# Three weight loads moved ahead of the last wait of a decode kernel

## The chip, the cores and the metric

The kernel runs on one core of a Trainium2 chip. The metric is the device time of one execution in microseconds (us); a profile's span is 2.0 to 2.6 us shorter than that time. PE is TensorE, the matrix engine; PEld are the weight loads (LDWEIGHTS) that the program has for its matmuls; ACT is ScalarE and DVE is VectorE. PSUM is where the program keeps the buffers that its matmuls write (`pm_r` here). Engines signal each other through semaphores. A ratio is the mean time of one kernel's runs over the mean of the other's runs of the same rounds, so it is not quite the ratio of the medians quoted beside it.

## The reference, cut to what matters

One token goes through an attention block over a cache of 65,536 keys and an MLP; both results and the token are added.

```python
xn = _layernorm(A_x)
return A_x + _A_ref(xn, A_k_cache, A_v_cache, A_wq, A_wo) + _B_ref(xn, B_w1, B_w2, B_w3, B_w4)
# _B_ref ends with:  h2 = _gelu(_layernorm(x1) @ w3) @ w4;  return x1 + h2      (w4: 3584 x 1024)
```

About 170 MB of caches and weights are read (169.87 MB on the page) for a result of 1024 numbers. The product with w4 comes last.

## The kernel before

Nearly all data come through one queue (169.87 of 170.03 MB), w4 last; its last four pieces get smaller (11, 5, 2 and 1 rows for each partition). So the last piece is one row of w4 for each partition. Its product is split over four column strips of the PE array (`tile_position=(0, 32 * q)`): two halves j of the result times two halves h of each. So one "row" is four weight loads and four matmuls of 256 columns. Strips 0 and 1 go to one PSUM buffer, read by ACT; strips 2 and 3 to another, read by DVE.

```python
    def narrow_rows(lo, hi):
        wt = st.tiles["w4"]
        for c in range(lo, hi):
            for h in range(2):
                for j in range(2):
                    q = 2 * h + j
                    nc.tensor.matmul(quarters[h][32 * q:32 * q + 32, 0:256], lhsT=hT[:, c:c + 1].to_broadcast([P, 32]),
                                     rhs=wt[:, D * c + 512 * j + 256 * h:D * c + 512 * j + 256 * (h + 1)], start=False, stop=False,
                                     tile_position=(0, 32 * q), skip_group_check=True)
    # ... (cut)
    nc.scalar.copy(out=out_t[:, 0, :], in_=quarters[0][0:64, 0:256])
    nc.vector.tensor_tensor(out=out_t[:, 1, :], in0=quarters[1][64:128, 0:256], in1=sums[1][:], op=ALU.add)
    nc.scalar.dma_start(out=out[0, 0, :].rearrange("(j n) -> j n", j=2), in_=out_t[31:33].rearrange("p h n -> p (h n)"))
```

On PE the last row stands as load 1, matmul 1 (waits for the last piece), load 2, matmul 2, load 3, matmul 3, load 4, matmul 4. Only matmul 1 has a wait.

Of the kernel before, what the change touches and what calls it, by code (L numbers as in the profile page):

```python
# [15 lines left out]
P = 128  # L16
# [12 lines left out]
def keep_loaded_weights(nc):  # L29




    for function in nc.m.functions:
        for block in function.blocks:
            held, kept = {}, []
            pe = [i for i in block.instructions if i.engine == mybir.EngineType.PE]
            user = dict(zip((i.name for i in pe), pe[1:]))
            for i in block.instructions:
                if i.engine == mybir.EngineType.PE:  # L40
                    if i.opcode == "Ldweights":
                        what = (i.tile_size, str(i.ins[0]))
                        waits = [j for j in (i, user[i.name]) if j.sync_info is not None and j.sync_info.on_wait]
                        if waits:
                            held.clear()
                        elif held.get(i.tile_position) == what and i.sync_info is None:
                            continue
                        if any(size != i.tile_size for size, _ in held.values()):
                            held.clear()
                        held[i.tile_position] = what  # L50
                    elif i.opcode != "Matmult" or i.ldweights is not False:
                        held.clear()
                kept.append(i)
            block.instructions = kept


# [41 lines left out]
def kernel(  # L98
# [13 lines left out]
):  # L112
    nc = tc.nc
    nc.at_finalize(keep_loaded_weights)
    nc.at_finalize(lead_with_the_first_load)
    nc.at_finalize(close_on_the_store)
    D = A_x.shape[-1]
# [413 lines left out]
    sums = [ogpool.tile([64, 256], F32, name="sums_a", tag="og"), ppool.tile([64, 256], F32, name="sums_b", tag="p")]  # L531
# [62 lines left out]
```

## Time and profile before

| | before |
|---|---|
| time, median of 3 runs (range) | 400.79 us (400.72 to 401.16) |
| span of the profiled execution | 398.6 us |
| end of the last transfer in the chain | 396.45 us |
| first matmul of the last row | 396.50 us |
| start of DVE's closing addition | 396.86 us |
| issue of the store | 397.36 us |

Everything the change can win lies between 396.50 and 396.86 us.

### The profile page before, as it was taken

To read this page: it belongs to the slowest core of one execution; us is meant where nothing else is said; L and a number is where in the kernel's file an instruction comes from. 1 tells how busy PE (TensorE), PEld (TensorE's weight loads), DVE (VectorE), ACT (ScalarE), POOL (GpSimd) and SP (SyncE) were. 2 spreads that over 40 slices of the span, in tenths; PEclk is the share of its full clock that TensorE was granted. 3 is DMA by queue.
4 is the path that set the end of the run, shared out by engine and by line. 5 is a ranking of instruction groups with operands and counts; after the bars stand their busy time and mean duration, and the time that the engine had idled before them with its cause. 6 is when DMAs were issued, how large, how long until landed. Compare 5 with 4: busy or idle time off the path is not lost.

```text
span 398.6 us, 2623 instructions
## 1 busy us (share of the span) xinstructions
PE 230.2 (58%) x1372; PEld 45.2 (11%) x862; DVE 211.5 (53%) x162; ACT 27.8 (7%) x36; POOL 10.0 (3%) x38
## 2 busy tenths in 40 slices
PE   0272970591569247834964297429553946394986
PEld 0210010000200010011001100101010102010142
DVE  0602010965196559643963696269449932894141
ACT  1002010003000200020002000200110020002000
POOL 2100000000000000000000000000000000002000
PEclk9998896697659686966895679678966986599999
DMA  9998999999999999999999999999999999999996
GB/s 421 421 443 382 439 441 480 434 427 421 416 428 427 434 460 442 427 427 421 427 429 427 467 434 434 423 421 427 441 429 441 454 427 388 418 455 431 409 427 260
DMA packets 4310, 170.03 MB, mean 427 GB/s; under 512 B 457, under 2 KB 459, under 8 KB 844
## 3 DMA queue, kind: packets, MB, share of 16 engines
q1 hardware_dynamic: 4294, 169.87, 98.9%
q8 instruction: 9, 0.15, 0.2%
q14 instruction: 1, 0.01, 0.0%
q10 hardware_dynamic: 6, 0.00, 0.0%
HBM read 169.87 MB, written 0.00 MB: 426 GB/s over the span
## 4 chain that ended last, share of the span: by engine, by line
DMA 54%; DVE 21%; PE 18%; ACT 2%; another core or an unknown queue 2%; SPq 1%; POOLq 1%; issue 1%; DVEq 0%; ACTq 0%
DMA big<-in_A_k_cache_dram 41%; DVE big L387 15%; PE sc L392 11%; DMA big<-in_B_w_dram 7%; DMA big<-in_A_wq_dram 6%; PE oacc L442 4%; DVE p_sb L413 2%; DVE mx L397 2%; PE psq L307 2%; ACT p_sb L410 2%; SPq L194 1%; POOLq L589 1%; ACT L410 0%; PE pm_mx L399 0%
## 5 line engine op out<-in xcount | busy, mean ns | idle before, releaser
L392 PE MATMUL sc<-big,qdiag 128*128 128x512 bf16 x512 | 128.5, 411 | 65.8 <-DVE big L387 65.6
L387 DVE STREAM_TRANSPOSE big<-big 128x4096 f32<-128x4096 f32 x32 | 139.4, 4412 | 48.0 <-DMA big<-in_A_k_cache_dram 48.0
L442 PE MATMUL oacc<-big,p_sb 128*32 128x512 bf16 x512 | 44.0, 520 | 34.5 <-DVE p_sb L413 34.5
L397 DVE TENSOR_REDUCE mx<-sc 128x1 f32<-128x2048 f32 x8 | 18.3, 2291 | 29.7 <-PE sc L392 29.7
L392 PEld LDWEIGHTS <-qdiag 128*128 128x128 bf16 x128 | 13.1, 102 | 176.6 <-issue 145.2
L410 ACT ACTIVATE p_sb<-sc,nball 128x2048 bf16<-128x2048 f32 x8 | 15.7, 1967 | 219.4 <-DVE nball L408 219.4
L413 DVE STREAM_TRANSPOSE p_sb<-p_sb 128x2048 bf16<-128x2048 bf16 x8 | 18.5, 2311 | 18.0 <-ACT p_sb L410 18.0
L442 PEld LDWEIGHTS <-p_sb 128*32 128x32 bf16 x512 | 16.8, 126 | 59.1 <-DVE p_sb L413 35.1
L451 DVE SCALAR_TENSOR_TENSOR og<-oacc,wb,og 128x512 f32<-128x512 f32 x4 | 3.0, 750 | 28.7 <-PE oacc L442 28.7
L307 PE MATMUL psh<-big,ln_rep_b 128*32 128x512 bf16 (+1 forms) x64 | 12.4, 942 | 4.0 <-DMA big<-in_B_w_dram 4.0
L485 PE MATMUL o_acc<-big,oT 128*1 128x512 bf16 x48 | 11.9, 413 | 2.4 <-ACT p_sb L410 2.4
L399 PE MATMUL pm_mx<-ident_f,mx 128*1 128x128 f32 x8 | 2.3, 283 | 19.1 <-DVE mx L397 19.1
L307 PE MATMUL psq<-big,ln_rep_a 128*32 128x512 bf16 x64 | 8.9, 445 | 4.1 <-DMA big<-in_A_wq_dram 4.1
L348 DVE STREAM_TRANSPOSE h_row<-h_row 128x896 bf16<-128x896 bf16 x1 | 1.1, 1111 | 17.2 <-ACT h_row L347 17.2
L332 POOL COPY qdiag<-qx 32x32 bf16<-32x32 bf16 x16 | 3.2, 203 | 262.8 <-PE sc L392 246.0
L250 PE MATMUL pm_ln<-ln_rowsum_a,ones_f 128*128 128x1 f32 x2 | 0.6, 348 | 12.5 <-DVE ln_rowsum_a L248 12.5
L320 DVE CAST q_row<-psq 64x1024 bf16<-64x1024 f32 x1 | 1.2, 1217 | 11.9 <-PE psq L307 11.9
L236 PE MATMUL psB<-big,hT 128*32 128x512 bf16 x46 | 5.5, 380 | 2.6 <-DMA big<-in_B_w_dram 2.6
L241 DVE STREAM_TRANSPOSE x_t<-x_row 32x256 bf16<-32x256 bf16 x4 | 2.5, 615 | 8.1 <-DMA x_row<-in_A_x_dram 8.0
L464 PE MATMUL pm_e<-ol,sel8big 128*128 128x129 f32 x6 | 1.8, 385 | 7.9 <-DVE ol L462 7.9
L406 PE MATMUL pm_mx<-ident_f,rep 1*128 1x1 f32 x8 | 1.9, 234 | 5.0 <-DVE rep L403 5.0
L448 ACT COPY og<-oacc 128x512 f32<-128x512 f32 x4 | 2.3, 585 | 33.5 <-PE oacc L442 24.4
(112 smaller groups left out, 77.1 us busy)
## 6 DMA issues: line engine op xcount, KB each, us to landing
big<-in_A_wo_dram SPq DMA_DIRECT2D x1, 8192.0 KB
big<-in_B_w_dram SPq DMA_DIRECT2D x1, 7168.0 KB
big<-in_B_w_dram SPq DMA_DIRECT2D x3, 2048.0 KB
big<-in_B_w_dram SPq DMA_DIRECT2D x1, 2816.0 KB
big<-in_B_w_dram SPq DMA_DIRECT2D x1, 1280.0 KB
big<-in_B_w_dram SPq DMA_DIRECT2D x1, 512.0 KB
big<-in_B_w_dram SPq DMA_DIRECT2D x1, 256.0 KB
big<-in_A_k_cache_dram SPq DMA_DIRECT2D x8
```

Of the source, the lines that this page charges most:

```text
L194: go(out=t[i0:i0 + 4 * k:4, WHOLE * D:(WHOLE + m) * D].rearrange("e (i n) -> e i n", i=m), in_=w4_v[m0:m0 + k * m, WHOLE, :].rearrange("(i ...
L236: return nc.tensor.matmul(psB[32 * j:32 * j + 32, :], lhsT=lhsT.to_broadcast([lhsT.shape[0], 32]), rhs=rhs, start=start, stop=False, tile_ ...
L307: nc.tensor.matmul(acc[32 * q:32 * q + 32, i, 0:n], lhsT=rep[:, c, :], rhs=cols(c, i, q), start=(c == 0), stop=(c == DC - 1), tile_positio ...
L332: nc.gpsimd.tensor_copy(out=qdiag[at, LEAD:].rearrange("p (x c) -> p x c", x=4)[:, :, 32 * a:32 * a + 8], in_=qx[at, :, 8 * g:8 * g + 8])
L387: nc.vector.transpose(out=words, in_=words)
L392: nc.tensor.matmul(sc[:, e, :], lhsT=qdiag[:, c0:c0 + P], rhs=cols[:, s, e, :, b2, :, r], start=(s == 0 and b2 == 0 and r == 0), stop=(s = ...
L397: nc.vector.reduce_max(out=mx[:], in_=sc[:].rearrange("p e n -> p (e n)"), axis=AX.X)
L410: nc.scalar.activation(out=p_sb[:], in_=sc[:], func=ACTF.Exp, bias=nball[:, b:b + 1], scale=SCALE, accum_out=group["lall"][:, b:b + 1])
L413: nc.vector.transpose(out=flat, in_=flat)
L442: mm = nc.tensor.matmul(oacc[32 * q:32 * (q + 1), :], lhsT=pT[:, e, 32 * t:32 * (t + 1)], rhs=vt[:, :, e, t, :], start=(e == 0 and t < 4), ...
L485: nc.tensor.matmul(tail["rows"][0:1, h2, :], lhsT=oT[g][:, j:j + 1], rhs=wt[:, g, j, 512 * h2:512 * (h2 + 1)], start=(g == 0 and j == 0), ...
L589: with _tile.TileContext(nc) as tc:
```

## The change

Its intent: have the weights of the last row in the array when its data land, so that nothing but the matmuls is left to do then. It edits the finished list of instructions: the loads of matmuls 2, 3 and 4 are put ahead of matmul 1. The other engines' instructions stay as they were.

```diff
+def load_last_row_ahead(nc):
+    for function in nc.m.functions:
+        for block in function.blocks:
+            pe = [i for i in block.instructions if i.engine == mybir.EngineType.PE and i.opcode in ("Ldweights", "Matmult")]
+            if len(pe) < 8:
+                continue
+            row = pe[-8:]
+            loads, sums = row[::2], row[1::2]
             ... (three assertions cut)
+            moved = {i.name for i in loads[1:]}
+            kept = []
+            for i in block.instructions:
+                if i.name == sums[0].name:
+                    kept += loads[1:]
+                if i.name not in moved:
+                    kept.append(i)
+            block.instructions = kept
...
     nc.at_finalize(keep_loaded_weights)
+    nc.at_finalize(load_last_row_ahead)
```

More of the change, by code (lines that the diff above doesn't have):

```diff
@@ L53, in keep_loaded_weights @@
                 kept.append(i)
+            block.instructions = kept
[7 more added lines that the diff above has]
+            loads, sums = row[::2], row[1::2]
+            assert all(i.opcode == "Ldweights" and i.sync_info is None for i in loads)
+            assert all(i.opcode == "Matmult" and i.tile_size == (P, 32) for i in sums)
+            assert sorted(i.tile_position for i in loads) == [(0, 32 * q) for q in range(4)]
+            moved = {i.name for i in loads[1:]}
[5 more added lines that the diff above has]
+                    kept.append(i)
             block.instructions = kept
```

## The prediction

The forecast's sum came to 12 ns, from 282.5 - 270.5 ns, with a range of 9 to 17. An allowance for PE's queue went into the upper end: it was not worked out from a trace. "Computed end" is the end of a matmul in the records, which is modelled, as the profile reader's own help says.

> **What bounds the kernel now.** I read the page's first parts, then the chain of work that ended last, then the timeline of the last five microseconds, then the single line that the change touches in narrow windows. The page says that the transfer queue is full from beginning to end:
>
> ```profile
> span 398.6 us, 2623 instructions
> PE 230.2 (58%) x1372; PEld 45.2 (11%) x862; DVE 211.5 (53%) x162; ACT 27.8 (7%) x36; POOL 10.0 (3%) x38
> DMA  9998999999999999999999999999999999999996
> HBM read 169.87 MB, written 0.00 MB: 426 GB/s over the span
> ```
>
> PE and DVE are a little over half busy; the DMA row is at 8 or 9 tenths in every slice but the last. The kernel is a stream of 170 MB with a short tail behind the last byte. The chain shows how long that tail is:
>
> ```profile
> 366.62 17.77 DMA big<-in_B_w_dram
> 384.38 0.02 issue
> 384.40 12.05 DMA big<-in_B_w_dram
> 396.45 0.04 issue
> 396.50 0.34 PE pm_r L553 x4
> 396.84 0.02 issue
> 396.86 0.42 DVE out_t L562
> ```
>
> The columns are start, length and what it was. From 366.62 to 396.45 us the chain is transfer of w4 alone. Then come four matmuls of line 553 (the last w4 row), the closing addition on DVE, and behind it the store of the result. So the time after 396.45 us is serial: about 2.15 us to the end of the span at 398.6. A nanosecond saved on PE there is a nanosecond of the total; a nanosecond saved on PE before 396.45 is worth nothing. The change acts at exactly this place, so its sign is not in much doubt; the question is its size. The timeline of the tail:
>
> ```profile
> 395.54 0.73 PE L553 MATMUL pm_r<-big,hT 128*32 128x256 bf16 x12
> 395.87 0.20 PEld L553 LDWEIGHTS <-hT 128*32 128x32 bf16 x8 [0.23 <-issue]
> 396.50 0.29 PE L553 MATMUL pm_r<-big,hT 128*32 128x256 bf16 x4 [0.23 <-DMA big<-in_B_w_dram]
> 396.50 0.10 PEld L553 LDWEIGHTS <-hT 128*32 128x32 bf16 x3 [0.43 <-issue]
> 396.82 0.36 ACT L561 CAST out_t<-pm_r 64x256 bf16<-64x256 f32 x1 [2.35 <-PE pm_r L553]
> 396.86 0.42 DVE L562 TENSOR_TENSOR out_t<-pm_r,sums_b 64x256 bf16<-64x256 f32 x1 [1.95 <-PE pm_r L553]
> 397.36 0.26 ACTq L563 DMA_DIRECT2D out_dram<-out_t  x1
> ```
>
> What to see: of the last row's four weight loads, one was done in the earlier group of eight, and three stand at 396.50, beside the four matmuls, after the wait for the DMA. That is the order of the program: load, waiting matmul, load, matmul, load, matmul, load, matmul. PE's load side sat idle for 0.43 us before these three, with nothing to wait for but the matmul in front of them. Note that four matmuls take 0.29 us together, not four times 0.28: each uses a quarter of the array's columns and they run side by side.
>
> [...]loads of a row stand inside the matmuls of the row before. [...]three loads did not pass a matmul that was still waiting for its semaphore. [...]the trace records 92 to 97 ns for each[...].
>
> **The change part by part.** It removes no instruction and adds none; the order of instructions on PE differs in the last eight alone. The words of the change speak of four loads, but the first stood in front of the waiting matmul already; three move. After it, PE has four loads in a row, then the waiting matmul and three more matmuls with nothing between. Loads and matmuls of the row before write and read the same strips of the array, but the first of the four loads shows already that this is no obstacle: it is among the loads that ended well before 396.50.
>
> The cost of a late load is read from matmul lengths. Line 553 in three windows (the order is minimum, median and maximum in ns): the last row; a stretch in the middle, where three rows run with their weights loaded during the row before; and the stretch just behind the previous wait, where the first three matmuls are a waiting one and two with late loads:
>
> ```profile
> L553 PE MATMUL pm_r<-big,hT x4: 269/282/283, 396.5 to 396.5; 128*32 128x256 bf16 x4
> L553 PE MATMUL pm_r<-big,hT x12: 272/272/273, 395.3 to 395.5; 128*32 128x256 bf16 x12
> L553 PE MATMUL pm_r<-big,hT x3: 269/283/283, 395.9 to 395.9; 128*32 128x256 bf16 x3
> ```
>
> A matmul whose weights are in place takes 269 to 273 ns; one whose load was issued just in front of it takes 282 to 283. So the late load costs 282.5 - 270.5 = 12 ns, not 92[...]. And the three late loads cost this once and not three times, because the four matmuls run side by side, some 3 ns apart (four in 0.01 us). The row ends with its last matmul: now 0.01 + 0.282 = 0.29 us after 396.50, as the timeline has it; after the change 0.01 + 0.271 = 0.28 us. [...]Sum: 12 ns, between 9 and 17.
>
> All of this is on the path: ACT (396.82) and DVE (396.86) wait for this row, DVE's addition ends at 397.28, the store is issued at 397.36. So these shift by the same 0.012 us. Nothing after it has a slot or grid to fall into that the profile would show. Weight loads that move forward land in the idle 0.43 us and cost nothing.
>
> Result: 400.79 - 0.012 = 400.78 us, a gain of 0.003%. The three times of before are 400.72, 400.79 and 401.16, a spread of 0.44 us, nearly forty times the expected gain. It can't be seen in the times; only the profile could show it.
>
> **The rivals.**
> (a) A late load is exposed in full. The recorded load is 92 ns, and computed ends could hide a stall of that length; three staggered loads took 0.10 us. The gain would be up to 0.09 us and the time 400.70. Against it: behind the last matmul of psB, whose weights were loaded ahead, ACT's copy of psB started 0.04 us after the computed end (394.06 to 394.10). Behind this row ACT started 0.03 us after the computed end (396.79 to 396.82). A hidden stall of 90 ns would make the second gap 0.09 us longer. I give this one chance in fifteen.
> (b) Nothing at all: the waiting matmul blocks the loads wherever they stand, or the queue executes the loads only when the matmuls using them are near. Against it: the row's first load ran ahead of the wait. It would leave 400.79. One chance in ten.
> (c) It gets slower: four loads back to back into strips still in use by the previous row hold up that row. The previous row ends by about 396.28 and the last data come at 396.45, so there is 0.17 us of slack for it; the time would not move. One chance in thirty that it costs anything[...].
> (d) Another wait takes over: DVE's addition needs sums_b too (done at 394.92), and the store needs ACT's half, which ended at 397.18 while DVE's ended at 397.28. None comes within 0.012 us of taking over, so the whole gain passes through.
> (e) The last landing itself moves. It ends a stream of 170 MB; 0.1% of that is 0.4 us and is the spread seen in the three runs. This swamps everything above and is why the range is what it is, in both directions.
>
> **Range and chances.** All the rivals lie within 0.1 us of each other; the range comes from (e). [...]Taking the seen spread of 0.44 us on both sides of the prediction as the estimate for a median from another set of executions gives 400.4 to 401.2. For a change of over 2% the time would have to move by 8 us, when the whole serial tail after the last landing is 2.15 us: even removing it could not do that. So within 2% is all but certain.
>
> **What would show it right or wrong.** In the profile of the changed kernel, the timeline must have no weight loads of the last line at or after the final wait; the load group before it has eleven (or eight and three). The last four matmuls should all be 269 to 273 ns with a maximum no longer at 283, and the row's busy time 0.28 instead of 0.29 us. From the row's start to DVE's start should be 0.35 us instead of 0.36 (ACT 0.31 instead of 0.32). If that distance falls to 0.28, rival (a) holds and my 12 ns is an artefact of computed ends. If loads still stand at the wait, (b) holds. If the row before ends later than the last landing, (c) holds. A total off by more than 0.4 us would mean that the landing of the last bytes moved, which should show in the chain as a different end of the DMA part, with the tail behind it unchanged.

## More of the kernel before

Matmul 2 signals ACT, matmul 4 signals DVE (300 and 342 ns after the start of matmul 1).

## The result, and the profile after

The changed kernel took 400.77 us (median of 6 runs, 400.45 to 401.17), the kernel before 400.81 us (6 runs, 400.72 to 401.16). The ratio is 0.9999 with a 95% interval from 0.9986 to 1.0012: the same time. The interval is about 1 us wide, so the times alone can't tell a gain of some nanoseconds from none.

The profile can, as long as one measures from the last row's first matmul and not from the span's start, since the row itself starts when the data land (0.04 us after the end of the chain's last transfer in both profiles), and that moves from execution to execution. First the chain of the changed kernel (start, length, what):

```profile
366.51 17.77 DMA big<-in_B_w_dram
384.29 0.02 issue
384.30 12.20 DMA big<-in_B_w_dram
396.50 0.04 issue
396.54 0.32 PE pm_r L575 x4
396.86 0.02 issue
396.89 0.43 DVE out_t L584
```

It has the same pieces as before. PE's piece went from 0.34 to 0.32 us, but the transfers ended at 396.50 instead of 396.45 us, which by itself took more than that. Then the timeline of the changed kernel's end (start, length, engine, line, instructions, and in brackets the idle time before and what ended it; lines are 22 further down in the changed file, so L553 is now L575):

```profile
395.91 0.23 PEld L575 LDWEIGHTS <-hT 128*32 128x32 bf16 x11 [0.24 <-issue]
396.54 0.27 PE L575 MATMUL pm_r<-big,hT 128*32 128x256 bf16 x4 [0.23 <-DMA big<-in_B_w_dram]
396.85 0.37 ACT L583 CAST out_t<-pm_r 64x256 bf16<-64x256 f32 x1 [2.35 <-PE pm_r L575]
396.89 0.43 DVE L584 TENSOR_TENSOR out_t<-pm_r,sums_b 64x256 bf16<-64x256 f32 x1 [1.93 <-PE pm_r L575]
397.39 0.27 ACTq L585 DMA_DIRECT2D out_dram<-out_t  x1
```

The group of eight loads has become eleven and no load stands at 396.54. All eleven are over by 396.14 us, 0.40 us ahead of the row's first matmul. The same four matmuls by line (minimum, median and maximum length in ns):

```profile
L575 PE MATMUL pm_r<-big,hT x4: 269/269/269, 396.5 to 396.5; 128*32 128x256 bf16 x4
```

Before, this read 269/282/283. In the trace's records, which have nanoseconds, ACT's copy starts 311 ns after the row's first matmul instead of 322, DVE's addition 345 instead of 366, and the store is issued at 849 instead of 867. So DVE starts 21 ns earlier, and 18 ns of that reach the store. The span ends 2107 ns after the row's first matmul instead of 2123, so 16 ns earlier.

### The profile page after: what moved, and what is told of

Its sections match the earlier page's. It is cut to its first block, busy times and chain, and to the rows that moved or that the text cites. A ratio compares the mean times of both kernels' runs of the same rounds, so it can differ in the third digit from the quotient of the medians.

```text
span 398.6 us, 2623 instructions
## 1 busy us (share of the span) xinstructions
PE 233.9 (59%) x1372; PEld 45.1 (11%) x862; DVE 211.5 (53%) x162; ACT 27.8 (7%) x36; POOL 10.1 (3%) x38
## 4 chain that ended last, share of the span: by engine, by line
DMA 54%; DVE 21%; PE 18%; ACT 2%; another core or an unknown queue 2%; SPq 1%; issue 1%; POOLq 1%; DVEq 0%; ACTq 0%
DMA big<-in_A_k_cache_dram 41%; DVE big L409 15%; PE sc L414 11%; DMA big<-in_B_w_dram 8%; DMA big<-in_A_wq_dram 5%; PE oacc L464 4%; PE psq L329 2%; DVE p_sb L435 2%; DVE mx L419 2%; ACT p_sb L432 2%; SPq L216 1%; POOLq L611 1%; ACT L432 0%; DVE m L423 0%
## 5 line engine op out<-in xcount | busy, mean ns | idle before, releaser
L414 PE MATMUL sc<-big,qdiag 128*128 128x512 bf16 x512 | 130.5, 417 | 64.2 <-DVE big L409 64.1
L507 PE MATMUL o_acc<-big,oT 128*1 128x512 bf16 x48 | 12.9, 439 | 2.4 <-ACT p_sb L432 2.4
L329 PE MATMUL psq<-big,ln_rep_a 128*32 128x512 bf16 x64 | 9.9, 486 | 3.9 <-DMA big<-in_A_wq_dram 3.9
```

What stands on the lines that cost most here:

```text
L329: nc.tensor.matmul(acc[32 * q:32 * q + 32, i, 0:n], lhsT=rep[:, c, :], rhs=cols(c, i, q), start=(c == 0), stop=(c == DC - 1), tile_positio ...
L414: nc.tensor.matmul(sc[:, e, :], lhsT=qdiag[:, c0:c0 + P], rhs=cols[:, s, e, :, b2, :, r], start=(s == 0 and b2 == 0 and r == 0), stop=(s = ...
L507: nc.tensor.matmul(tail["rows"][0:1, h2, :], lhsT=oT[g][:, j:j + 1], rhs=wt[:, g, j, 512 * h2:512 * (h2 + 1)], start=(g == 0 and j == 0), ...
```

## The experiments

The question is no longer whether the time moved; it didn't. It is whether the 21 ns are real, which of the three loads they come from, and whether they would show in the time if they were large. The records' nanoseconds are counted from the last row's first matmul. "Signal" is the semaphore update of matmul 2 (for ACT) or matmul 4 (for DVE), which is recorded apart from the computed end of the matmul; from that end to the update of matmul 4 it took 14 to 70 ns in these runs.

| run | late loads | signal to ACT | signal to DVE | ACT starts | DVE starts | store issued |
|---|---|---|---|---|---|---|
| before | 2, 3, 4 | 300 | 342 | 322 | 366 | 867 |
| before_again | 2, 3, 4 | 300 | 343 | 323 | 365 | 867 |
| after | none | 287 | 321 | 311 | 345 | 849 |
| after_again | none | 287 | 321 | 310 | 343 | 846 |
| all_late | 1, 2, 3, 4 | 305 | 347 | 327 | 370 | 873 |
| last_late | 4 | 287 | 326 | 310 | 348 | 852 |
| first_late | 2 | 300 | 335 | 323 | 358 | 859 |
| late_x5 | 2, 3, 4, five times each | 373 | 449 | 396 | 472 | 975 |
| early_x5 | none, 12 extra loads ahead | 288 | 322 | 311 | 346 | 849 |

### Both kernels once more

Edit: none.

> The changed kernel once more, with five timed rounds. Theory A (a load issued behind the wait delays the row's end and what waits for it, and nothing else moves): in the profile the last row takes 0.27 us and DVE's addition starts 0.34 to 0.35 us after the row's first matmul, as in the first profile of the changed kernel; the time lies within 0.2% of the kernel before and the interval holds 1.000. Rival B (the 18 to 20 ns between the first two profiles are chance of one execution): DVE's start is again 0.36 to 0.37 us after the row's start.

> The kernel before once more, for a second profile. Theory A: last row 0.29 us, its matmuls 269/282/283 ns, DVE's addition 0.36 to 0.37 us after the row's first matmul. Rival B: anything from 0.34 to 0.37.

Measured: the second profiles repeat the first within 2 ns at DVE's start (343 and 365 ns) and within 1 ns at the signals. Theory A of this run holds, and chance (B) is out. (In the runs below, A is a narrower theory: a late load lengthens its own matmul only.) The times, from five rounds: 400.75 us (400.57 to 401.06) against 400.88 us (400.43 to 401.29), ratio 0.9998, interval 0.9984 to 1.0012. The single look at the kernel before took 400.56 us, faster than the changed kernel's median: its last row began at 396.34 us, 0.15 us earlier than in the first profile, and its span was as much shorter. The four profiles of the two kernels put that row's start between 396.34 and 396.54 us: a spread of 0.2 us, ten times the gain.

### All four loads late

`again` builds a weight load with the same operands and strip as the given one; 0 keeps its name. The lines that move the loads are taken out.

```diff
+    # load 1 is built anew with the wait of matmul 1 on it
+    waits = sums[0].sync_info.on_wait
+    kept = [again(i, 0, waits) if i.name == loads[0].name else i for i in block.instructions]
```

> The wait for the last piece is put on the row's first load too, so that all four loads run behind it. Theory A (each late load lengthens only its own matmul by 12 to 14 ns, beside the others): the first matmul goes from 269 to 282 ns, but the row still ends with its fourth, 0.29 us after the start, and DVE starts 0.36 to 0.37 us after the first matmul; the first load stands 2 ns ahead of it. Rival C (late loads add up in the queue, a few ns each): DVE's start comes 4 to 6 ns later than in the kernel before. Rival D (a load's recorded 92 ns are exposed when nothing is done ahead): 0.09 us later.

Measured: ACT and DVE start 4 to 5 ns later than in the kernel before, which is what rival C expected; 0.09 us (rival D) is far off. Matmul 1 lengthened to 283 ns, as A has it; C says nothing of lengths. A alone, with its 0.36 to 0.37 us, can't be told from this reading at its upper edge; the next two runs decide.

### Only the fourth matmul's load late

```diff
-                    kept += loads[1:]
+                    kept += loads[1:3]
```
(and the same slice in `moved`)

> Two of the three loads are moved, the one of the fourth matmul stays behind the wait. Theory A (the row ends with its last matmul, whose own load counts): fourth matmul 282 to 283 ns and started some 2 ns after the third, so nearly the whole gain is lost: DVE 0.355 to 0.36 us after the row's start, that is 4 ns less than before, which is the queue time of two loads. ACT's copy, which waits for the second matmul, keeps its gain (0.31 us). Rival C (the loads add up): two thirds of the gain are kept, DVE at 0.35 us.

Measured, by line, the last row of this run:

```profile
L575 PE MATMUL pm_r<-big,hT x4: 269/269/282, 396.5 to 396.5; 128*32 128x256 bf16 x4
L575 PEld LDWEIGHTS <-hT x1: 92/92/92, 396.5 to 396.5; 128*32 128x32 bf16 x1
```

One matmul has 282 ns, the fourth, and it started at 7 ns (10 in the kernel before, 5 in the changed one, so some 2 ns for each late load). Its computed end is thus 289 ns, only 3 less than the 292 of the kernel before (10 + 282). But its signal came at 326 instead of 342, and DVE started at 348 ns: 16 to 18 of the 21 ns were kept. Theory A falls. The row doesn't end with the fourth matmul's own load, and the computed ends, on which A was built, were off: from computed end to signal it is 50 ns in the kernel before and 37 ns here. Rival C's number, 0.35 us, was met, but not its rule: equal shares would have kept 14 ns.

### Only the second matmul's load late

```diff
-                    kept += loads[1:]
+                    kept += loads[2:]
```
(and the same slice in `moved`)

> Only the load of the second matmul stays behind the wait, those of the third and fourth are moved. The run with only the last load late kept 17 of the 21 ns (DVE 0.348 us after the row's start, between 0.366 and 0.344), which speaks against the row ending with its own last late load. Theory E (one late load stalls the matmuls behind it too[...], and further late loads mostly run beside that stall): ACT 0.322 to 0.323 us as in the kernel before, and DVE at 0.355 to 0.358 us although its own matmuls had their weights, some 12 ns behind the changed kernel. Theory A (only its own load delays a matmul): ACT 0.322, DVE 0.343 to 0.346 us.

Measured, from the timeline of this run:

```profile
396.46 0.29 PE L575 MATMUL pm_r<-big,hT 128*32 128x256 bf16 x4 [0.24 <-DMA big<-in_B_w_dram]
396.47 0.09 PEld L575 LDWEIGHTS <-hT 128*32 128x32 bf16 x1 [0.41 <-issue]
396.79 0.37 ACT L583 CAST out_t<-pm_r 64x256 bf16<-64x256 f32 x1 [2.35 <-PE pm_r L575]
396.82 0.42 DVE L584 TENSOR_TENSOR out_t<-pm_r,sums_b 64x256 bf16<-64x256 f32 x1 [1.93 <-PE pm_r L575]
```

DVE needs matmuls 3 and 4, whose weights were in place, and still its signal came at 335 ns, 14 later than in the changed kernel, while ACT's came 13 later. So this late load delayed its own matmul's signal and that of matmul 4, two places behind it. Matmul 4's computed length is 269 ns, as in the changed kernel, and it signals 35 ns after matmul 2 (34 there). In all nine runs of the table its signal follows that of matmul 2, by 34 to 76 ns. What holds it back is not shown. Theory E's numbers were met. The gain of 21 ns at DVE's signal is then 13 to 14 for load 2 and 7 to 8 for loads 3 and 4 on top of it; load 4 alone is 5. Why a single late load costs 14 ns at matmul 2 and 5 at matmul 4 is not shown. Load 3 alone was not tried.

### More loads, behind and ahead of the wait

```diff
 # late_x5 and late_x41, in the kernel before: each of loads 2, 3, 4 is followed by 4 (40) copies of itself
+                if i.name in {j.name for j in loads[1:]}:
+                    kept += [again(i, len(kept) * 100 + n) for n in range(4)]
 # early_x5, in the changed kernel: the same 12 copies ahead of matmul 1
+                    kept += [again(j, 100 * x + n) if n else j for x, j in enumerate(loads[1:]) for n in range(5)]
```

> In the kernel before, each of the three late loads is issued five times in a row (twelve more loads behind the wait, same values). It measures the rate of loads on the path. [...]If only the few ns of issue count: 0.04 us longer. If the recorded 92 ns count in full: 1.1 us longer.

> In the changed kernel the three moved loads are issued five times, all ahead of the wait (the same twelve extra loads). Theory A (what stands ahead of the wait is free while it fits in the idle 0.43 us): last row 0.27 us and DVE 0.345 us after the row's start, as in the changed kernel, whatever they cost. Rival (loads ahead of the wait are only executed when the row starts): as in the run with the extra loads behind the wait.

> As the run with five, but each late load 41 times, so 120 more loads on the path, to make the delay large against the spread of the times. If what PE does behind the last landing passes one to one into the time: the time rises by exactly what the row and DVE's start are later in the profile; [...]at 3 ns 0.4 us (401.2), at 92 ns 11 us (411.8). If part of it is hidden by something that the chain doesn't show, the time rises by less than DVE's start.

The rates from the texts of late_x5 and late_x41 are 3 ns a load, an estimate from the kernel before, where the three late loads start at 1, 5 and 8 ns, and the recorded 92 ns.

Measured, from the timelines, first with twelve extra loads behind the wait (late_x5), then with the same twelve ahead of it (early_x5):

```profile
396.57 0.38 PE L580 MATMUL pm_r<-big,hT 128*32 128x256 bf16 x4 [0.24 <-DMA big<-in_B_w_dram]
396.57 0.19 PEld L580 LDWEIGHTS <-hT 128*32 128x32 bf16 x15 [0.43 <-issue]
397.04 0.43 DVE L589 TENSOR_TENSOR out_t<-pm_r,sums_b 64x256 bf16<-64x256 f32 x1 [2.04 <-PE pm_r L580]
...
395.99 0.30 PEld L582 LDWEIGHTS <-hT 128*32 128x32 bf16 x23 [0.22 <-issue]
396.61 0.27 PE L582 MATMUL pm_r<-big,hT 128*32 128x256 bf16 x4 [0.22 <-DMA big<-in_B_w_dram]
396.95 0.43 DVE L591 TENSOR_TENSOR out_t<-pm_r,sums_b 64x256 bf16<-64x256 f32 x1 [1.91 <-PE pm_r L582]
```

Behind the wait, DVE starts at 472 ns, 106 later, so 8.8 ns for each extra load on average. That is more than the estimate of 0.04 us for all twelve and far less than the 1.1 us of the recorded 92 ns. Ahead of the wait it starts at 346 ns, as in the changed kernel (345): all 23 loads are over by 396.29 us, 0.32 us before the row begins. What stood ahead of the last wait was free here.

With 120 extra loads the delay is large enough for the times. The timeline of that run:

```profile
396.55 0.27 PE L580 MATMUL pm_r<-big,hT 128*32 128x256 bf16 x1 [0.22 <-DMA big<-in_B_w_dram]
396.56 2.12 PEld L580 LDWEIGHTS <-hT 128*32 128x32 bf16 x123 [0.42 <-issue]
...
398.95 0.43 DVE L589 TENSOR_TENSOR out_t<-pm_r,sums_b 64x256 bf16<-64x256 f32 x1 [3.95 <-PE pm_r L580]
```

123 loads took 2.12 us, and DVE starts 2.40 us after the row's first matmul instead of 0.37, so 2.03 us later, or 17 ns for each extra load on average. The span's end is also 2.03 us further from the row's start (4.15 instead of 2.12 us). The time was 403.21 us (402.86 to 403.28, 4 runs) against 400.66 (400.57 to 401.38, 7 runs), ratio 1.0060, interval 1.0044 to 1.0077. That is 1.8 to 3.1 us, and 2.03 lies in it. (The medians differ by 2.55 us; the spans of the same runs, 400.5 to 401.2 against 398.5 to 398.9, by 2.1 us in the mean.) So this delay of PE behind the last landing reached the end of the span in full, and the time agrees with that. Neither rate in the expectations, 3 or 92 ns a load, was the measured one.

The records of both runs show where the averages, 8.8 and 17 ns, part. ACT's signal shows what the extra loads in front of matmul 2 cost: four moved it from 300 to 373 ns, forty to 1034, which is 18 ns for each in both runs. What DVE's signal lost beyond that is due to the loads in front of matmuls 3 and 4: 34 ns for eight of them (4 each), but 1295 ns for eighty (16 each). In the first run eight of the ten loads of matmuls 3 and 4 ran beside those of matmul 2: when matmul 2 started, at 76 ns, 13 of the 15 loads had started, and only five are its own. In the second, 46 of the 123 loads had started when matmul 2 did, at 737 ns, of which 41 are its own. So loads for other strips ran beside a strip's own here: eight had started by matmul 2 in one run, five in the other.

### A version with unequal halves

In the changed kernel ACT finished its half at 677 ns and DVE at 772, and the store waits for both: ACT issues it at 849 ns, after a wait for DVE's semaphore that ends at 810. This version gives ACT 296 of each 512 columns and DVE 216.

```diff
+CUT = (0, 296, 512)
+    wide = [CUT[1], 512 - CUT[1]]
-    nc.scalar.copy(out=out_t[:, 0, :], in_=quarters[0][0:64, 0:256])
-    nc.vector.tensor_tensor(out=out_t[:, 1, :], in0=quarters[1][64:128, 0:256], in1=sums[1][:], op=ALU.add)
+    nc.scalar.copy(out=out_t[:, 0:CUT[1]], in_=quarters[0][0:64, 0:wide[0]])
+    nc.vector.tensor_tensor(out=out_t[:, CUT[1]:512], in0=quarters[1][64:128, 0:wide[1]], in1=sums[1][:], op=ALU.add)
 ... (the matmuls and copies that fill these buffers, cut at the same column)
```

> A version that the runs point to: since what stands behind the last landing passes one to one, the changed kernel with its last two parallel copies made unequal. ACT now takes 296 of each 512 columns and DVE 216 (256 each before), because ACT ends its half 0.09 us before DVE. From the trace ACT needs 0.86 ns a column (0.366 us for 256, 0.585 for 512) and DVE about 1.2, so ACT's end should come 0.03 to 0.05 us later (0.71 to 0.73 us after the row's start), DVE's 0.03 to 0.05 us earlier (0.72 to 0.74 instead of 0.77), and the store's issue at 0.80 to 0.82 instead of 0.847. In the time 0.04 us, 400.7, not to be told from the kernel before by the times (ratio 0.9998, interval with 1.000 in it).

```profile
396.55 0.40 ACT L585 CAST out_t<-pm_r 64x296 bf16<-64x296 f32 x1 [2.14 <-PE pm_r L577]
396.58 0.38 DVE L586 TENSOR_TENSOR out_t<-pm_r,sums_b 64x216 bf16<-64x216 f32 x1 [1.77 <-PE pm_r L577]
397.04 0.27 ACTq L587 DMA_DIRECT2D out_dram<-out_t  x1
```

The row's first matmul is at 396.22 us here. ACT ends 725 ns after it, DVE 746, and the store is issued at 822 ns instead of 846 to 849: another 25 ns, at the edge of the expected 0.80 to 0.82 us. DVE's addition is 42 ns shorter (384 instead of 426), but it starts 17 ns later (362), which I had left out. That is what 40 more columns in the first two matmuls cost in the computed length too (286 instead of 269 ns); DVE's matmuls stand behind them in the program. The time was 400.59 us (400.44 to 400.66, 5 runs) against 400.66 (400.43 to 401.11, 9 runs), ratio 0.9998, interval 0.9984 to 1.0012. In the trace it beats both kernels by 25 and 45 ns at the store's issue; in the times it is the same.

## Why the prediction was right or wrong

- **The time, the range and the chances** were right: 400.78 us was predicted, in a range of 400.4 to 401.2, and 400.77 us measured. They would have been right without any gain, as the prediction says of its step (e), so they speak for no mechanism. That the landing of the last bytes sets the scatter, as (e) has it, is not shown. The row's start moved from 396.34 to 396.54 us in four profiles; but five of the changed kernel's six runs have the same span, 398.6 us, and took 400.71 to 401.17 us. Most of that scatter lies outside the profiled span.
- **The path.** That this row ends the kernel and that PE's time passes through one to one was right. It is shown at the small scale by the store's issue (18 to 21 ns earlier) and the span's end (16 and 17 ns in the two pairs of profiles) and at the large by the run with 120 loads (2.03 us later at DVE, 2.03 us later at the end).
- **The loads ahead are free.** Right: eleven loads in the earlier group as foretold, and twelve more ahead of the wait still cost nothing (DVE's start at 346 ns against 345).
- **The size, 12 ns, was too small.** The signal to DVE and its start moved by 21 to 22 ns, outside the stated 9 to 17. The term that was mis-sized is "the three late loads cost this once and not three times, because the four matmuls run side by side", together with "the row ends with its last matmul". Measured, load 2 alone delays the last signal by 14 ns though matmul 4 had its weights, and loads 3 and 4 add 7 to 8. The matmuls start side by side, but they don't finish so: matmuls 2 and 4 start 7 ns apart before and 4 after, and signal 42 and 34 ns apart. What the allowance for PE's queue stood for is seen in the starts: the four matmuls start within 5 ns of each other with the loads ahead and within 10 ns before. But even that accounts only for the computed ends, which went from 292 to 274 ns, 18 earlier.
- **The check by release gaps.** The prediction took 0.03 us from computed end to ACT's start as proof that the computed ends could be trusted. That excluded a stall of 90 ns, rightly (rival (a) is refuted by DVE's start at 0.345 and not 0.28 us). It could not vouch for 10 ns, and ACT waits for matmul 2 and not for the row's end, from which the gap was taken: the distance from the computed end of matmul 4 to its signal is 50 ns before, 47 after, 37 with only its own load late and 60 with only load 2 late (275 to 335). In the run with 120 extra loads, where matmul 4 starts long after matmul 3 has ended, it is 14 ns (2357 to 2371).
- **Rivals (b) and (c)** are refuted: the loads ran ahead of the wait (395.91 to 396.14 us), and the row started 0.04 us after the end of the transfer in the chain, as before. **Rival (d)** was right as put: ACT ends 0.09 us before DVE, no other wait took over.
- **The profile's signs** came as foretold but for the row's busy time, 0.27 instead of 0.28 us.

What stays open: why a single late load costs less at matmul 4 than at matmul 2, how many loads can run ahead of a matmul that is held up (eight in one run, five in the other), and how the array splits the 13 ns of a single late load between loading and waiting. The runs show the sizes and not the mechanism inside PE.

## What to carry to other kernels

Before valuing a change, find what ends last and measure from there: here the whole prize was the stretch from the last landing to the store, and a gain of 21 ns could be read from a row's first matmul to its reader's start although the times of the kernel before scatter over nearly 1 us (400.43 to 401.38 in all rounds). Put everything that doesn't need the last data ahead of the last wait; here twelve extra loads cost nothing there and some 4 to 18 ns each behind it. The order in the program counted: in the two profiles of the kernel before, the load side stood idle for 0.43 and 0.44 us with three loads behind a matmul that waited. For differences of tens of nanoseconds trust the start of what waits and not the length of a matmul: from matmul 4's computed end to its signal it was 14 ns with 120 extra loads and 70 with twelve behind the wait.
